# Batch 0's head: both halves' maxima turned, the second sum in its scores' bank, the first products mixed

## The chip, the cores and the metric

The kernel runs on one core of a Trainium2 chip. The metric is the device time of one execution in microseconds (us); a version is told by the median of several runs. Engines are named as in the profile: PE is TensorE's products (PEld its weight loads), DVE is VectorE, ACT is ScalarE, POOL is GpSimd, SP is SyncE, which issues DMAs only.

## What is computed

Two cross attentions between a sequence and a small state, for 8 batches of 8 heads, feed a feed-forward layer with a leaky ReLU.

```python
# x: (8, 8, 512, 64), state: (8, 8, 32, 64)
scores = scale * x @ state.T               # per batch and head: 512 x 32
a = exp(scores - scores.max(-1)); a /= a.sum(-1) + 1e-9
xread = a @ state                          # 512 x 64
scores2 = scale * state @ x.T              # 32 x 512
a2 = exp(scores2 - scores2.max(-1)); a2 /= a2.sum(-1) + 1e-9
sread = a2 @ x                             # 32 x 64
rows = concatenate([xread, sread], axis=2) # per batch 544 rows of 8*64 = 512
h = rows @ w_in                            # 512 x 2048
out = max(0.01 * h, h) @ w_out             # 2048 x 512
```

The sequence rows and the state rows go through the feed-forward layer apart. The sequence part is regrouped: `M = state @ w_in` is formed per batch (256 x 2048: 8 heads of 32 state rows, in two groups of 128 partitions), and the hidden layer is `M.T @ a`, so that xread itself is never formed.

## The kernel before, in words

All loops are unrolled in Python, and each engine executes its instructions in the order in which the code writes them; an engine that waits holds up all that is behind it in its queue. There is no scheduler that moves instructions.

**Tiles.** One core has eight PSUM banks of 128 partitions x 512 fp32. The code names them by tag: `ph` and `py` have two single banks each, `sc` and `big` are one pair of banks each. A tile that is asked for under a tag takes the next buffer of the tag, and its first write waits until the readers of the tile that was there are done.

**Batch 0's head** (lines 490 to 673) is written by hand, because nothing else can fill the engines while the first inputs arrive. Its steps, by the functions that the change touches:

- `spin` (L172): seven idle products on a tile of zeros.
- `x0_t(q)` (L505), q = 0 to 3: batch 0's x, cast by VectorE (L150), is transposed by four products against the identity; ScalarE copies the result to `xT` (L508). For q > 0, `zeros_in` (L498) first puts one 256-column product of zeros into the same bank.
- `scores0(q)` (L519): scores with sequence positions on partitions, 64 columns for each of the four blocks of positions. `max0(q)` (L548, VectorE) takes their maxima over the 32 states, negated.
- A "half" u is four heads. `split0` (L558, L560, VectorE) writes half u's maxima as a sum of two bf16 parts into `parts[u]`.
- `rows0(u)` (L530): the same scores once more, now with (head, state) on partitions and positions on columns, into the tile `scn[u]` under `ph`: four products of 32 output partitions each.
- The negated maxima are added onto `scn[u]` by products. For half 0 `turn0` (L566) turns the 32 columns of parts into 32 rows with one product, ScalarE copies them to `mt` (L571), and `spread_turned` (L576) adds them with four products against a selector. For half 1 `spread0` (L538) spreads each part with 16 products of 32 output partitions, 32 in all, straight from `parts[1]`.
- `exp0(u)` (L583, ScalarE) takes the exponential of `scn[u]`.
- `open_sums` (L589) writes the small constant 1e-9 into both halves' sums, which lie in two banks of one tile under `big`; `sum0(u)` (L596) adds the exponentials over the states with four products; `recip0(u)` (L604, VectorE) takes the reciprocal.
- `recip0_rows(u)` (L538 again) spreads the reciprocals over the state rows with 16 products into a tile `qb0[u]` under `ph`, and `probs0(u)` (L612, VectorE) multiplies: `aT[:, u]`, the probabilities.
- `a_m(a, c, tag)` (L400): one quarter (512 of 2048 columns) of M, 8 products. ScalarE copies out quarter 0 of batch 0 (L670) and of batch 1 (L412), VectorE quarter 1 of both (L414), and for batch 0 quarters 2 and 3 in halves (`m_halves`, L707).

**Batch 0's first products** (L686): for each pair j of the 16 blocks of 128 hidden columns four products, over two groups g and two blocks v, in the order g outside and v inside, into two banks under the tags ph, py, big, ph, py, ph, py, big; ScalarE applies the leaky ReLU (L694, L698). Between pairs stand quarters 2 and 3 of batch 0's M and batch 0's second scores (L264).

**Output products** (`piece`, L449) multiply a block of hidden columns by `w_out`. Batch 0's first ones are interleaved with batch 1's transposes (L743), its scores (L264) and quarters 2 and 3 of its M, which both use the two `ph` banks and are copied out by ScalarE (L412).

After this head, the other batches run in one loop in which TensorE's first products (L421) and output products (L449) alternate.

Of the kernel before, what the change touches and what calls it, by code (L numbers as in the profile page):

```python
# [9 lines left out]
P = 128  # L10
# [17 lines left out]
def kernel(  # L28
# [466 lines left out]

    def zeros_in(flat, n, w):
        for _ in range(n):
            nc.tensor.matmul(flat[:, :w], lhsT=idle[:, :P], rhs=idle[:, :w], start=True, stop=True)  # L498

    def x0_t(q):  # L500
        ps = psum.tile([P, NT, P], FP32, name="pxth", tag=("ph", "py")[q // 2])
        if q:
            zeros_in(ps[:].rearrange("p t c -> p (t c)"), 1, S // 2)
        for t in range(NT):
            nc.tensor.matmul(  # L505
                ps[:, t, :], lhsT=pair_of(a0, t, q), rhs=ident[:], start=True, stop=True
            )
        SCA(a0.xT[:, :, q, :], ps[:])  # L508
# [18 lines left out]
    def rows0(u):  # L527
        scn[u] = psum.tile([P, S], FP32, name="scn", tag="ph")
        for c in range(NK):
            nc.tensor.matmul(  # L530
                scn[u][NS * c:NS * (c + 1), :], lhsT=stbd[:, 2 * u + c // 2, c % 2, :],
                rhs=a0.xT[:, :, 2 * u + c // 2, :], start=True, stop=False,
            )

    def spread0(dst, part, start, stop):
        for t in range(NT):
            for c in range(NK):
                nc.tensor.matmul(  # L538
                    dst[NS * c:NS * (c + 1), P * t:P * (t + 1)],
                    lhsT=part[:, t, c:c + 1].to_broadcast([P, NS]),  # L540
                    rhs=ident[:], start=start, stop=start or (stop and t == NT - 1),
                )
# [20 lines left out]

    def turn0():
        pt = psum.tile([NR, P], FP32, name="pmt", tag="py")
        nc.tensor.matmul(  # L566
            pt[:], lhsT=parts[0][:].rearrange("p t s c -> p (t s c)"), rhs=ident[:],
            start=True, stop=True,
        )
        mt = consts.tile([NR, P], BF16, name="mt")  # L570
        SCA(mt[:], pt[:])  # L571
        return mt

    def spread_turned(dst, mt):
        for t in range(NT):
            nc.tensor.matmul(  # L576
                dst[:, P * t:P * (t + 1)], lhsT=sel[:NR, t].rearrange("r c n -> r (c n)"),
                rhs=mt[:], start=False, stop=t == NT - 1,
            )
# [4 lines left out]

    def open_sums():
        rs = psum.tile([P, 2, S], FP32, name="r0", tag="big", bufs=1)
        for u in range(2):
            r0[u] = rs[:, u, :NG]
            nc.tensor.matmul(  # L589
                r0[u], lhsT=nc.const_aps.tensor(1.0, (2, P), BF16), rhs=eps[:],  # L590
                start=True, stop=False,
            )

# [13 lines left out]
    def recip0_rows(u, q):  # L607
        qb0[u] = psum.tile([P, S], FP32, name="qb0", tag="ph")
        spread0(qb0[u], q[:].rearrange("p (t c) -> p t c", t=NT), True, True)

# [40 lines left out]
    max0(3)  # L651
    mt = turn0()
    rows0(1)
    open_sums()
    split0(m0[1], parts[1][:, :, 0], parts[1][:, :, 1])
    spread_turned(scn[0], mt)
    exp0(0)
    for i in range(2):
        spread0(scn[1], parts[1][:, :, i], False, i == 1)
    exp0(1)  # L660
    pm, pm1 = a_m(a0, 0, "sc"), a_m(a1, 0, "py")
    sum0(0)
    q = [recip0(0)]
    sum0(1)
    q.append(recip0(1))
# [35 lines left out]

    def m_halves(a, c, tag):
        pm = a_m(a, c, tag)
        for i in range(2):
            part = slice(2 * P * i, 2 * P * (i + 1))
            cols = slice(DM * c + 2 * P * i, DM * c + 2 * P * (i + 1))
            VEC(a.M[:, :, cols], pm[:, :, part])  # L707

    for j, tag in enumerate(("ph", "py", "big", "ph", "py", "ph", "py", "big")):
        j *= 2  # L710
        t, bk = open_ff1_0(tag)
        for g in range(2):
            ff1_0(bk, j, g)
        relu0(t, j)
        if j == 4:
            m_halves(a0, 2, "sc")
        elif j == 8:
            a_scores(a0)
            m_halves(a0, 3, "big")
            a_max2(a0)  # L720
# [214 lines left out]
```

## Time and profile before

| | |
|---|---|
| median of 3 runs | 214.61 us (214.38 to 214.87) |
| profiled execution, its own time | 214.58 us |
| its span, first to last instruction | 212.2 us |
| TensorE busy in the span | 205.7 us |
| ScalarE, VectorE, GpSimd busy | 138.4, 99.3, 26.6 us |
| batch 0's first product of the 16 blocks starts | 12.80 us |

The profile is of one execution. A row of the timeline gives the start and the length of a run of equal instructions, the engine, the line of the kernel, the operation, output and inputs by the program's names, the shapes and the count; in brackets stands the idle time of the engine just before, and what ended it. Single durations within such a run overlap, since products are pipelined. The chain of waits follows the work that ended last back from the end, at each step to what released it or to the instruction before it on its engine. A few records of products can be missing, so a count can be one short.

### The profile page before, as it was taken

What the parts mean: (1) busy time and instruction counts of PE and PEld (TensorE: products, weight loads), DVE (VectorE), ACT (ScalarE), POOL (GpSimd) and SP (SyncE); (2) the same over time, 40 slices, a digit from 0 to 9 for tenths busy, and PEclk for the clock granted to TensorE, in tenths of its full rate; (3) what the DMA queues carried; (4) which work ended last, traced back from release to release, by engine and by line L of the source; (5) the groups of instructions that cost most, each with busy time, mean ns of one, the idle gap of its engine ahead of it and who ended that gap; (6) DMA issues with size and microseconds to landing.
All of it is one profiled execution on the core that took longest, in us unless ns stands there. A gap on an engine that the chain in (4) does not pass through costs nothing.

```text
span 212.2 us, 3638 instructions
## 1 busy us (share of the span) xinstructions
PE 205.7 (97%) x1456; PEld 97.0 (46%) x1481; DVE 99.3 (47%) x148; ACT 138.4 (65%) x265; POOL 26.6 (13%) x40
## 2 busy tenths in 40 slices
PE   7989999999999999999999999999999999999994
PEld 2543444343554444444444445444444445466543
DVE  4777795896857055832684096604592000000001
ACT  3679656997787477856686569648884656464420
POOL 8814200030032050530000000000000000000000
PEclk9999999999999999999999999999999999999999
DMA  6999999974973986497117221422115210111123
GB/s 190 208 207 296 255 252 153 314 166 87 246 200 86 209 229 222 100 285 112 49 53 150 50 100 53 109 39 102 49 49 99 88 61 2 49 49 53 49 49 99
DMA packets 38415, 27.68 MB, mean 130 GB/s; under 512 B 24576, under 2 KB 33152, under 8 KB 38400
## 3 DMA queue, kind: packets, MB, share of 16 engines
q1 hardware_dynamic: 32624, 18.75, 34.8%
q0 software_dynamic: 5392, 8.39, 17.9%
q10 hardware_dynamic: 384, 0.33, 0.8%
q8 instruction: 11, 0.18, 0.3%
q14 instruction: 4, 0.03, 0.1%
HBM read 17.30 MB, written 8.91 MB: 124 GB/s over the span
## 4 chain that ended last, share of the span: by engine, by line
PE 94%; DMA 2%; issue 1%; DVE 1%; ACT 0%; DVEq 0%
PE py L449 50%; PE ph L421 23%; PE pm L400 4%; PE ph L432 3%; PE pyw L449 3%; PE ph L686 3%; PE psr L373 2%; DMA xf<-in_x_dram 2%; PE pyh L474 2%; PE sc L264 1%; PE php L686 1%; PE pxth L505 1%; DVE aT L612 0%; PE pxt L743 0%; DVE xb L150 0%
## 5 line engine op out<-in xcount | busy, mean ns | idle before, releaser
L449 PE MATMUL py<-w_out_bf,hT 128*128 128x512 bf16 x445 | 116.7, 379 | 0.9
L426 ACT ACTIVATE hT<-ph 128x512 bf16<-128x512 f32 x112 | 66.4, 601 | 39.1 <-PE ph L421 39.1
L449 PEld LDWEIGHTS <-hT 128*128 128x128 bf16 x496 | 46.9, 98 | 56.9 <-issue 4.9
L421 PE MATMUL ph<-aT,M 128*128 128x512 bf16 x223 | 65.2, 379 | 0.1
L421 PEld LDWEIGHTS <-M 128*128 128x128 bf16 x224 | 21.8, 98 | 27.0 <-issue 1.4
L458 ACT COPY ysb<-py 128x512 f32<-128x512 f32 x31 | 18.1, 585 | 12.3 <-PE py L449 11.6
L274 DVE TRANSPOSE_TENSOR_REDUCE mrow<-sc 128x32 f32<-128x1024 f32 x7 | 8.8, 1250 | 33.9 <-PE sc L264 33.9
L479 DVE COPY ysh<-pyh 128x384 f32<-128x384 f32 x1 | 0.6, 558 | 48.1 <-PE pyh L474 48.1
L143 POOL CAST xb<-xl 128x2048 bf16<-128x2048 f32 x5 | 9.5, 1891 | 55.9 <-DMA xl<-in_x_dram 45.1
L296 DVE TRANSPOSE_TENSOR_REDUCE r<-e 128x32 f32<-128x1024 bf16 x7 | 8.7, 1245 | 11.2 <-ACT e L291 11.2
L414 ACT CAST M<-pm 128x1024 bf16<-128x1024 f32 x11 | 11.1, 1011 | 1.1 <-PE pm L400 0.7
L330 ACT ACTIVATE e<-sc,mcol 128x512 bf16<-128x512 f32 x16 | 11.1, 698 | 0.0
L414 DVE CAST M<-pm 128x1024 bf16<-128x1024 f32 x9 | 10.8, 1216 | 0.0
L324 DVE TENSOR_REDUCE mcol<-sc 128x2 f32<-128x1024 f32 x8 | 9.7, 1215 | 0.0
L436 ACT ACTIVATE hs<-ph 128x256 bf16<-128x256 f32 x16 | 6.0, 385 | 4.6 <-PE ph L432 4.4
L305 DVE STREAM_TRANSPOSE qb<-qh 128x1024 bf16<-128x1024 bf16 x7 | 8.7, 1246 | 0.2
L282 DVE STREAM_TRANSPOSE mrowb<-mrow 128x1024 f32<-128x1024 f32 x7 | 8.7, 1245 | 0.2
L284 DVE TENSOR_TENSOR sh<-sc,mrowb 128x1024 f32<-128x1024 f32 x7 | 8.6, 1225 | 0.2
L432 PE MATMUL ph<-sr_t,w_in_bf 128*128 128x256 bf16 x64 | 8.3, 273 | 0.0
L449 PE MATMUL pyw<-w_out_bf,hT 128*128 128x512 bf16 x30 | 7.8, 379 | 0.1
L400 PE MATMUL pm<-w_in_bf,st_t 64*32 64x512 bf16 x192 | 7.6, 379 | 0.0
L291 ACT ACTIVATE e<-sh 128x1024 bf16<-128x1024 f32 x7 | 7.4, 1053 | 0.3 <-DVE sh L284 0.3
(107 smaller groups left out, 159.2 us busy)
## 6 DMA issues: line engine op xcount, KB each, us to landing
out_dram<-ysb SPq DMA_DIRECT2D x31, 256.0 KB, 2.3
xl<-in_x_dram SPq DMA_DIRECT2D x3, 1024.0 KB, 6.5
w_in_bf<-in_moe_w_in_dram POOLq DMA_DIRECT2D x4, 512.0 KB, 9.4
xl<-in_x_dram POOLq DMA_DIRECT2D x2, 1024.0 KB, 6.4
w_out_bf<-in_moe_w_out_dram POOLq DMA_DIRECT2D x6, 256.0 KB, 12.6
xf<-in_x_dram SPq DMA_DIRECT2D x4, 256.0 KB, 4.0
x<-in_x_dram POOLq DMA_DIRECT2D x2, 512.0 KB, 13.9
xl<-in_x_dram POOLq DMA_DIRECT2D x2, 512.0 KB, 13.8
```

What stands on the lines that cost most here:

```text
L143: nc.gpsimd.tensor_copy(xt[b][:].rearrange("p t h d -> p h t d"), xl[b][:].rearrange("p h (t d) -> p h t d", t=NT),)
L274: nc.vector.tensor_reduce(out=m1[:], in_=flat.rearrange("p (c j) -> p c j", j=NS), axis=AX.X, op=ALU.max, apply_transpose=True,)
L282: nc.vector.transpose(m1b[:], m1[:, :, None].to_broadcast([P, n, NS]))
L324: nc.vector.tensor_reduce(out=a.m2[:], in_=a.sc[:], axis=AX.X, op=ALU.max, negate=True)
L330: nc.scalar.activation(out=a.e2[:, g], in_=a.sc[:, g, :], func=AF.Exp, bias=a.m2[:, g:g + 1], accum_out=a.r2[:, g:g + 1],)
L400: nc.tensor.matmul(at[v][NS * r:NS * (r + 1)], lhsT=st_of(a, g, k), rhs=w_in_bf[D * g:D * (g + 1), k, DM * c:DM * (c + 1)], start=True, st ...
L414: copy(a.M[:, :, cols], pm[:])
L421: nc.tensor.matmul(ph[:], lhsT=a.M[:, g, P * j:P * (j + 1)], rhs=a.aT[:, g, :], start=(g == 0), stop=(g == 1),)
L426: nc.scalar.activation(out=hT[:, j, :], in_=ph[:], func=AF.Prelu, scale=1 / SCALE, alpha=0.01)
L432: nc.tensor.matmul(ph[:, :n], lhsT=w_in_bf[:, k, P * j:P * (j + 1)], rhs=sr_t[:, k, :], start=(k == 0), stop=(k == NK - 1),)
L449: nc.tensor.matmul(y.py, lhsT=hT[:, j, P * i:P * (i + 1)], rhs=w_out_bf[:, j, :], start=(j == 0), stop=(j == 15),)
L458: copy(ysb[:], ys[b, i].py)
```

## The change

Four edits, all in batch 0's head and the work just behind it:

1. `zeros_in` and its three products go. `rows0` writes 64 output partitions with each product, two for a half instead of four.
2. Half 1's maxima take the path of half 0's: `turn0(1)` (one product), a copy to a second `mt` tile, by VectorE, and `spread_turned(scn[1], ...)` (four products), in place of 32 products. TensorE does all of this before the sums.
3. The sums are opened one by one. Half 0's is opened and summed, and its reciprocal taken, before M's quarter 0 of batches 0 and 1 (16 products, which stood ahead of it). Half 1's sum is put into `scn[1]`, the bank of the scores that its exponential has read, and comes behind those 16 products.
4. Batch 0's first products are ordered anew: pairs 0 and 2 are opened together, pair 6 has one product ahead of M's quarter 2, the pairs from 8 on go v outside and g inside. Quarter 2 of M is copied out in parts of 128, 128 and 256 columns. Of the output products, the two of row block 3 over the first two hidden blocks go ahead of batch 1's second transposes, and the second two hidden blocks of row block 1 go ahead of batch 1's scores.

In all, TensorE then has 34 products and 34 weight loads fewer. VectorE has two instructions more (the copy and the extra part of quarter 2); the queues of ScalarE, GpSimd and SP keep their order and count.

```diff
-    def zeros_in(flat, n, w):
-        for _ in range(n):
-            nc.tensor.matmul(flat[:, :w], lhsT=idle[:, :P], rhs=idle[:, :w], start=True, stop=True)
-
     def x0_t(q):
         ps = psum.tile([P, NT, P], FP32, name="pxth", tag=("ph", "py")[q // 2])
-        if q:
-            zeros_in(ps[:].rearrange("p t c -> p (t c)"), 1, S // 2)
...
     def rows0(u):
         scn[u] = psum.tile([P, S], FP32, name="scn", tag="ph")
-        for c in range(NK):
+        for v in range(2):
             nc.tensor.matmul(
-                scn[u][NS * c:NS * (c + 1), :], lhsT=stbd[:, 2 * u + c // 2, c % 2, :],
-                rhs=a0.xT[:, :, 2 * u + c // 2, :], start=True, stop=False,
+                scn[u][D * v:D * (v + 1), :],
+                lhsT=stbd[:, 2 * u + v].rearrange("p g n -> p (g n)"),
+                rhs=a0.xT[:, :, 2 * u + v, :], start=True, stop=False,
             )
...
-    def turn0():
+    def turn0(u, copy):
         pt = psum.tile([NR, P], FP32, name="pmt", tag="py")
         nc.tensor.matmul(
-            pt[:], lhsT=parts[0][:].rearrange("p t s c -> p (t s c)"), rhs=ident[:],
+            pt[:], lhsT=parts[u][:].rearrange("p t s c -> p (t s c)"), rhs=ident[:],
             start=True, stop=True,
         )
-        mt = consts.tile([NR, P], BF16, name="mt")
-        SCA(mt[:], pt[:])
+        mt = consts.tile([NR, P], BF16, name=f"mt{u}")
+        copy(mt[:], pt[:])
         return mt
...
-    def open_sums():
-        rs = psum.tile([P, 2, S], FP32, name="r0", tag="big", bufs=1)
-        for u in range(2):
-            r0[u] = rs[:, u, :NG]
-            nc.tensor.matmul(
-                r0[u], lhsT=nc.const_aps.tensor(1.0, (2, P), BF16), rhs=eps[:],
-                start=True, stop=False,
-            )
+    def open_sum(u, bank):
+        r0[u] = bank[:, :NG]
+        nc.tensor.matmul(
+            r0[u], lhsT=nc.const_aps.tensor(1.0, (2, P), BF16), rhs=eps[:],
+            start=True, stop=False,
+        )
...
-    mt = turn0()
+    mt = [turn0(0, SCA)]
     rows0(1)
-    open_sums()
     split0(m0[1], parts[1][:, :, 0], parts[1][:, :, 1])
-    spread_turned(scn[0], mt)
+    spread_turned(scn[0], mt[0])
     exp0(0)
-    for i in range(2):
-        spread0(scn[1], parts[1][:, :, i], False, i == 1)
+    mt.append(turn0(1, VEC))
+    spread_turned(scn[1], mt[1])
     exp0(1)
-    pm, pm1 = a_m(a0, 0, "sc"), a_m(a1, 0, "py")
+    open_sum(0, psum.tile([P, 2, S], FP32, name="r0", tag="big", bufs=1)[:, 0])
     sum0(0)
     q = [recip0(0)]
+    pm, pm1 = a_m(a0, 0, "sc"), a_m(a1, 0, "py")
+    open_sum(1, scn[1])
     sum0(1)
     q.append(recip0(1))
...
-    def m_halves(a, c, tag):
+    def m_parts(a, c, tag, at):
         pm = a_m(a, c, tag)
-        for i in range(2):
-            part = slice(2 * P * i, 2 * P * (i + 1))
-            cols = slice(DM * c + 2 * P * i, DM * c + 2 * P * (i + 1))
+        for i in range(len(at) - 1):
+            part = slice(at[i], at[i + 1])
+            cols = slice(DM * c + at[i], DM * c + at[i + 1])
             VEC(a.M[:, :, cols], pm[:, :, part])
...
-    for j, tag in enumerate(("ph", "py", "big", "ph", "py", "ph", "py", "big")):
-        j *= 2
+    t0, b0 = open_ff1_0("ph")
+    t2, b2 = open_ff1_0("py")
+    ff1_0(b0, 0, 0, (0,))
+    ff1_0(b2, 2, 0)
+    ff1_0(b0, 0, 0, (1,))
+    ff1_0(b0, 0, 1)
+    ff1_0(b2, 2, 1)
+    relu0(t0, 0)
+    relu0(t2, 2)
+    t4, b4 = open_ff1_0("big")
+    for g in range(2):
+        ff1_0(b4, 4, g)
+    relu0(t4, 4)
+    t6, b6 = open_ff1_0("ph")
+    ff1_0(b6, 6, 0, (0,))
+    m_parts(a0, 2, "sc", (0, P, 2 * P, DM))
+    ff1_0(b6, 6, 1, (0,))
+    for g in range(2):
+        ff1_0(b6, 6, g, (1,))
+    relu0(t6, 6)
+    for j, tag in ((8, "py"), (10, "ph"), (12, "py"), (14, "big")):
         t, bk = open_ff1_0(tag)
-        for g in range(2):
-            ff1_0(bk, j, g)
+        for v in range(2):
+            for g in range(2):
+                ff1_0(bk, j, g, (v,))
...
     for u in range(2):
-        if u:
-            piece(0, h0, 2, 0, bank=wide[:, 0], js=half[0])
-        else:
-            for i in range(2):
+        for i in range(2):
+            if u:
+                piece(0, h0, 2 + i, 0, bank=wide[:, i], js=half[0])
+            else:
                 piece(0, h0, i, 0, js=half[0])
...
-    piece(0, h0, 3, 0, bank=wide[:, 1], js=half[0])
-    piece(0, h0, 0, 0, js=half[1])
+    for i in (0, 1):
+        piece(0, h0, i, 0, js=half[1])
     a_scores(a1)
     m_evict(a1, 2, a_m(a1, 2, "ph"), SCA)
...
-    for i in range(1, NT):
+    for i in (2, 3):
         piece(0, h0, i, 0, js=half[1])
```

More of the change, by code (lines that the diff above doesn't have):

```diff
@@ L528, in rows0, with spread0 @@
         scn[u] = psum.tile([P, S], FP32, name="scn", tag="ph")
-        for c in range(NK):
+        for v in range(2):
             nc.tensor.matmul(
-                scn[u][NS * c:NS * (c + 1), :], lhsT=stbd[:, 2 * u + c // 2, c % 2, :],
-                rhs=a0.xT[:, :, 2 * u + c // 2, :], start=True, stop=False,
+                scn[u][D * v:D * (v + 1), :],
+                lhsT=stbd[:, 2 * u + v].rearrange("p g n -> p (g n)"),
+                rhs=a0.xT[:, :, 2 * u + v, :], start=True, stop=False,
             )
-    def spread0(dst, part, start, stop):
+    def spread0(dst, part):
         for t in range(NT):
@@ L540, in spread0 @@
                     lhsT=part[:, t, c:c + 1].to_broadcast([P, NS]),
-                    rhs=ident[:], start=start, stop=start or (stop and t == NT - 1),
+                    rhs=ident[:], start=True, stop=True,
                 )
@@ L608, in recip0_rows @@
         qb0[u] = psum.tile([P, S], FP32, name="qb0", tag="ph")
-        spread0(qb0[u], q[:].rearrange("p (t c) -> p t c", t=NT), True, True)
+        spread0(qb0[u], q[:].rearrange("p (t c) -> p t c", t=NT))
     def probs0(u):
@@ L700, in relu0 @@
             )
-    def m_halves(a, c, tag):
+    def m_parts(a, c, tag, at):
         pm = a_m(a, c, tag)
-        for i in range(2):
-            part = slice(2 * P * i, 2 * P * (i + 1))
-            cols = slice(DM * c + 2 * P * i, DM * c + 2 * P * (i + 1))
+        for i in range(len(at) - 1):
+            part = slice(at[i], at[i + 1])
+            cols = slice(DM * c + at[i], DM * c + at[i + 1])
             VEC(a.M[:, :, cols], pm[:, :, part])
-    for j, tag in enumerate(("ph", "py", "big", "ph", "py", "ph", "py", "big")):
-        j *= 2
+    t0, b0 = open_ff1_0("ph")
[19 more added lines that the diff above has]
+    for j, tag in ((8, "py"), (10, "ph"), (12, "py"), (14, "big")):
         t, bk = open_ff1_0(tag)
-        for g in range(2):
-            ff1_0(bk, j, g)
+        for v in range(2):
+            for g in range(2):
+                ff1_0(bk, j, g, (v,))
         relu0(t, j)
-        if j == 4:
-            m_halves(a0, 2, "sc")
-        elif j == 8:
+        if j == 8:
             a_scores(a0)
-            m_halves(a0, 3, "big")
+            m_parts(a0, 3, "big", (0, 2 * P, DM))
             a_max2(a0)
```

## The prediction, made before the change was run

> **What bounds the kernel now.** The page comes first.
>
> ```profile
> span 212.2 us, 3638 instructions
> PE 205.7 (97%) x1456; PEld 97.0 (46%) x1481; DVE 99.3 (47%) x148; ACT 138.4 (65%) x265; POOL 26.6 (13%) x40
> PE 94%; DMA 2%; issue 1%; DVE 1%; ACT 0%; DVEq 0%
> ```
>
> TensorE is busy 97% of the span and carries 94% of the chain that ended last. So whatever makes TensorE stand still once, or start its long stream later, is paid at the end in full. The stream becomes dense at batch 0's first products, about 13.4 us in. The edits lie before that point and, for one pair of output products, near 25 us. The chain of waits through the head says what leads there:
>
> ```profile
> 5.74 0.21 PE pxth L498
> ...
> 6.81 0.21 PE pxth L498
> ...
> 9.66 0.56 PE scn L538 x32
> 10.22 0.56 PE pm L400 x16
> ```
>
> Columns: start, length, what. Nearly all the removed work (the fillers L498, the 32-fold spread L538) stands on this chain, so at first sight it looks like a gain of most of a microsecond. But a chain step on TensorE is only what TensorE did last before the next thing; whether something else was due at the same time has to be read from the order in time, engine by engine:
>
> ```profile
> 7.49 0.76 DVE L548 TENSOR_REDUCE m<-sct 128x8 f32<-128x256 f32 x2 [0.23 <-PE sct L519]
> ...
> 8.49 0.17 DVE L560 TENSOR_TENSOR parts<-m,parts 128x16 bf16<-128x16 f32 x1
> 8.58 0.75 DVE L548 TENSOR_REDUCE m<-scq 128x8 f32<-128x256 f32 x2
> ...
> 9.57 0.17 DVE L560 TENSOR_TENSOR parts<-m,parts 128x16 bf16<-128x16 f32 x1
> ...
> 11.59 0.26 DVE L604 RECIPROCAL q<-r 128x16 bf16<-128x16 f32 x1 [0.33 <-PE r L596]
> 12.02 1.29 DVE L612 TENSOR_TENSOR aT<-e,qb 128x512 bf16<-128x512 bf16 x2 [0.17 <-PE qb L538]
> 13.22 2.35 DVE L414 CAST M<-pm 128x1024 bf16<-128x1024 f32 x2
> ```
>
> Columns: start, length, engine, line, operation, tiles, count, and in brackets the idle time before it. From 7.49 to 9.74 no row notes idle time after the first: VectorE, not TensorE, decides when half 0's maxima (8.49 + 0.17 = 8.66) and half 1's (9.57 + 0.17 = 9.74) stand ready as parts.
>
> **The fillers and the wider score rows: nothing.**
>
> ```profile
> 5.13 0.61 PE L505 MATMUL pxth<-ident,xb 128*128 128x128 bf16 x4 [0.32 <-DVE xb L150]
> ...
> 6.42 0.40 PE L519 MATMUL sct<-stbd,xT 128*128 128x64 bf16 x4
> 7.16 0.29 PE L519 MATMUL sct<-stbd,xT 128*128 128x64 bf16 x4
> 7.39 0.39 PE L505 MATMUL pxth<-ident,xb 128*128 128x128 bf16 x4
> 8.49 0.29 PE L519 MATMUL scq<-stbd,xT 128*128 128x64 bf16 x4
> 8.71 0.23 PE L566 MATMUL pmt<-ident,parts 128*32 128x128 bf16 x1
> ...
> 9.29 0.38 PE L576 MATMUL scn<-mt,sel 32*128 32x128 bf16 x4
> ...
> 11.31 0.24 PE L596 MATMUL r<-zeroed,e 128*128 128x4 bf16 x4 [0.35 <-DVE q L604]
> ```
>
> Without the fillers the third transposes can be earlier by their 0.21 us, and the last score block (8.49 to 8.78) by about 0.1; but the reduction that reads it begins only as VectorE comes to it, at about 8.9. The reductions themselves start on the scores of 7.16, which wait for a ScalarE copy and not for a filler. The two 64-column products in place of four 32-column ones lie between the best case (side by side, one 0.22 pace as four take now) and one after the other (0.22 more); either ends ahead of the turned maxima, for which the four products of 9.29 wait (ScalarE's copy, 8.98 + 0.26 = 9.24, below). Cover gone, each would cost those 0.1 to 0.2 us. I take 0.
>
> **Half 1's maxima, turned instead of spread.** For half 0 the trace shows this whole path.
>
> ```profile
> 8.98 0.26 ACT L571 CAST mt<-pmt 32x128 bf16<-32x128 f32 x1 [0.58 <-PE pmt L566]
> 9.70 1.17 ACT L583 ACTIVATE e<-scn 128x512 bf16<-128x512 f32 x2 [0.47 <-PE scn L576]
> 11.71 1.10 ACT L412 CAST M<-pm 128x512 bf16<-128x512 f32 x2
> ```
>
> Parts ready at 8.66, exponential begun at 9.70: 1.04 us for a product, a copy, four products and the handovers. Half 1's copy goes to VectorE, and no row has VectorE copying 128 columns out of PSUM. Bounds: 0.26 (the reciprocal of 16 columns above) and 0.38 (half of the 0.76 of two reductions of 256). I take 0.29, near the lower, for 128 columns lie between; so 1.07. Half 1's exponential then starts at 9.74 + 1.07 = 10.81 and ends at 11.41. Today the two exponentials end together at 9.70 + 1.17 = 10.87. So half 1's is 0.54 us *later*: the spread was short (0.56 on the chain) and overlapped half 0's exponential, while the turned path is latency. Behind it on ScalarE wait the four M copies, which slide by the same 0.54: the last ends at 12.81 + 0.54 = 13.35.
>
> **Sums.** Today the second sum stands behind the first reciprocal: it starts at 11.31 after 0.35 of idle time, though its exponentials were ready at 10.87. In its own bank that wait goes, and it now waits for 11.41. Opening it (one small product into the bank that the exponential has just left) and getting into the sum's shape costs between 0.04 and 0.2; I take 0.16 with the handover, so 11.57. Behind the opener in TensorE's queue stand the second sum and the spreads of both reciprocals, half 0's too, and VectorE's two products of aT wait for those. From a sum's start to its reciprocal's end takes 11.85 − 11.31 = 0.54 today, hence 12.11 against 11.85: **0.26 later**. The first M quarter's 16 products (0.56) move behind the first sum; they run while half 1's exponential is under way, so they cost nothing, and if that cover were gone they would cost 0.56. The second opener moves along and no DMA does; SP's and GpSimd's queues stay in order.
>
> [...]
>
> **First products mixed.**
>
> ```profile
> 11.90 0.18 PEld L538 LDWEIGHTS <-q 128*32 128x32 bf16 x12 [0.19 <-DVE q L604]
> 12.80 0.39 PE L686 MATMUL ph<-aT,M 128*128 128x512 bf16 x1
> 13.36 1.67 PE L686 MATMUL ph<-aT,M 128*128 128x512 bf16 x6 [0.17 <-DVE aT L612]
> 14.87 1.03 PE L686 MATMUL php<-aT,M 128*128 128x512 bf16 x4
> ```
>
> From half 1's reciprocal on (11.85, with 0.05 of handover), TensorE runs through: spread 11.90, M quarter 1, first product 12.80. The second product needs the bank that aT's last step frees at 13.31, so TensorE loses 13.36 − 12.80 − 0.22 = **0.34**. In the changed order everything is 0.26 later: first product 13.06, two of pair 2 at 13.28 and 13.49 (their banks were copied out by 13.35), then half 0's other at 13.71, when aT (13.31 + 0.26 = 13.57) is long there. The 0.34 is gone. The pair read from the third pair of blocks is then due at 14.87 + 0.26 − 0.34 = 14.79; M quarter 1 is cast by 13.22 + 2.35/2 + 0.26 = 14.66, so it just fits. The first of quarter 2's narrower casts (a quarter of such a cast, 0.3, to the 0.38 above) has three products (0.65) ahead of its reader. The head: **−0.08 us**.
>
> **The output products moved.** Row block 3's two go ahead of batch 1's second transposes, and in their place row block 1's two come from behind batch 1's M quarter 2 to ahead of its scores:
>
> ```profile
> 24.58 0.40 PE L400 MATMUL pm<-w_in_bf,st 64*32 64x512 bf16 x8
> 24.91 0.60 PE L449 MATMUL py<-w_out_bf,hT 128*128 128x512 bf16 x2
> 25.35 0.81 PE L449 MATMUL pyw<-w_out_bf,hT 128*128 128x512 bf16 x3
> 26.31 0.41 PE L400 MATMUL pm<-w_in_bf,st 64*32 64x512 bf16 x8
> 25.04 1.07 ACT L412 CAST M<-pm 128x512 bf16<-128x512 f32 x2 [1.27 <-PE pm L400]
> ```
>
> Quarter 3 (26.31) uses the two banks that ScalarE empties by 25.04 + 1.07 = 26.11, that is 1.53 after quarter 2's start, 1.58 with the handover. Today six products (one record missing) fill 1.73. With four left, TensorE is there at 1.73 − 0.43 = 1.30 and waits 1.58 − 1.30 = **0.28**. Bounds: 0, if the first bank alone held it up (its second product needs the second bank, so I exclude it nearly), and 0.35. Batch 1's scores also come 0.43 later, but the work that follows has some 0.9 us before TensorE reads it at 34.6.
>
> ```profile
> 32.95 0.69 DVE L306 TENSOR_TENSOR aT<-e,qb 128x1024 bf16<-128x1024 bf16 x1
> 34.59 0.86 PE ph L421 x4
> ```
>
> **Sum**: −0.08 + 0.28 = +0.20 us on the profiled execution's 214.58 (span 212.2 and 2.4 around it), which is the runs' median 214.61 less 0.03: **214.8**. With the copy, the opener and the stall at their bounds: 214.3 to 215.0. Of this kernel 0.2% (0.43 us) can be told from nothing.
>
> **Rivals.** *The clock comes late* (slower). The four transposes take 0.61 at 5.13 and 0.39 at 7.39: TensorE goes at half pace until about 6.9.
>
> ```profile
> 3.40:6.90 3.50, 3.18 (x26) 1.60 (x25) 2.68 (x5) 1.50 (x4) 3.50 (x5) 1.00 1.10 306
> ```
>
> Columns: stretch, its length, busy time and count on PE, PEld, DVE, ACT and POOL, granted clock, DMA share, GB/s. TensorE is busy 3.18 of these 3.50 us, fillers included (the granted clock reads 1.00 throughout, so only the pace tells). Take 0.4 us of fillers away and full pace may come later. If it lasts past the last score block: 0.11 for the scores at 7.16, 0.22 for the transposes, 0.11 for scores, 0.21 for rows, less some 0.22 in which the block now lies ready or comes earlier: 0.43 more, **215.2**. For it: fillers do nothing else visible. Against: the share falls only by a tenth. [...]
>
> [...]
>
> *The chain is right* (faster): TensorE's count does set the head. Then fillers 0.42 and the spread 0.56 go, 0.23 and 0.38 for turning come back, and with the 0.34 the head gains 0.71; less 0.28 that is 0.43: **214.1**, or 213.9 if the later stall does not come. Against it stands VectorE's unbroken row until 9.74.
>
> *The head changes nothing and the stall does not appear*: 214.5.
>
> **How the numbers follow.** Forecast 0.38 (of it 0.07 beyond +0.43), late clock 0.24 (0.22), dearer path 0.17 (0.16), chain right 0.18 (0.16 at −0.43 or beyond), nothing 0.03. Faster 0.16, same 0.39, slower 0.45: no single case of slower is likelier than the forecast, but they add up. For 8 in 10 the range is 214.0 to 215.5, taking in most of each rival.
>
> **What would show it.** Half 1's exponential starting near 10.8 and its reciprocal ending near 12.1; no idle at the first products; the third pair of blocks' first product at about 14.8; quarter 3 of batch 1 waiting about 0.28 for ScalarE; transposes from 6.9 on still at 0.39 for four. A first M quarter ending before 10.8, or four transposes at 0.6 after 7.3, would prove the sum wrong.

## The result, and the profile after

The changed kernel took **217.11 us** (median of 6 runs, 215.91 to 218.04) against 214.54 (6 runs, 214.22 to 214.87) for the kernel before, measured beside it: ratio **1.0116, 95% interval 1.0075 to 1.0157**. Ratios here leave out runs more than 1.5% above their kernel's fastest, and those are often the very runs that lost the TensorE clock, so the experiments below also give the median over all runs and count the runs whose mean granted clock over the span is under 0.995.

The page of the changed kernel's profiled execution (217.19 us, span and instructions first; then busy time by engine, the granted clock in 40 slices, and the shares of the chain that ended last):

```profile
span 214.8 us, 3596 instructions
PE 209.7 (98%) x1447; PEld 97.6 (45%) x1447; DVE 100.2 (47%) x150; ACT 138.6 (65%) x265; POOL 26.3 (12%) x40
PEclk9979999999999999999999999999999999999999
PE 92%; DVE 4%; DMA 2%; ACT 0%; issue 0%; SPq 0%; ACTq 0%; DVEq 0%
```

TensorE has *fewer* instructions (34 by the code; the records show 1447 products for 1456, since some are missing, and 1447 weight loads for 1481) and is busy 4.0 us *longer* (209.7 for 205.7). More busy time with less work can only be slower work. The third slice of the clock, 10.7 to 16.1 us, shows a 7. Cut at the points where the clock changes (stretch, length, busy time and count on PE, PEld, DVE, ACT and POOL, granted clock, DMA share, GB/s):

```profile
9.77:13.18 3.41, 2.95 (x77) 1.82 (x83) 1.64 (x6) 2.57 (x5) 1.34 (x2) 1.00 1.24 207
13.18:16.59 3.41, 3.41 (x23) 1.05 (x8) 2.98 (x4) 1.05 (x3) 0.70 (x1) 0.50 1.24 207
16.59:20.00 3.41, 3.41 (x22) 1.15 (x20) 1.35 (x3) 3.41 (x8) 1.41 (x2) 1.00 1.10 338
```

The clock was released at 9.77 (before: about 6.9), was taken back for exactly one stretch of 3.41 us from 13.18, and then stayed. Ahead of the first release the column reads 1.00 whatever the pace, so there only the pace tells. TensorE in order of time (start, length, line, operation, tiles, count, and in brackets the idle time before):

```profile
7.35 0.61 PE L499 MATMUL pxth<-ident,xb 128*128 128x128 bf16 x4
...
9.87 0.39 PE L571 MATMUL scn<-mt,sel 32*128 32x128 bf16 x4
10.20 0.23 PE L561 MATMUL pmt<-ident,parts 128*32 128x128 bf16 x1
10.79 0.38 PE L571 MATMUL scn<-mt,sel 32*128 32x128 bf16 x4 [0.37 <-DVE mt L566]
...
13.23 0.68 PE L400 MATMUL pm<-w_in_bf,st 64*32 64x512 bf16 x8
13.84 3.24 PE L680 MATMUL ph<-aT,M 128*128 128x512 bf16 x8
16.92 1.03 PE L680 MATMUL php<-aT,M 128*128 128x512 bf16 x4
```

The transposes at 7.35 still take 0.61 for four, the half pace. The eight first products take 16.92 − 13.84 = 3.08 where 8 × 0.216 = 1.73 were due (0.216 is the median spacing of such products at full clock in this trace): +1.35 in one place. VectorE and ScalarE over the turned path:

```profile
9.90 0.17 DVE L555 TENSOR_TENSOR parts<-m,parts 128x16 bf16<-128x16 f32 x1
10.46 0.28 DVE L566 CAST mt<-pmt 32x128 bf16<-32x128 f32 x1 [0.39 <-PE pmt L561]
...
12.33 0.26 DVE L597 RECIPROCAL q<-scn 128x16 bf16<-128x16 f32 x1 [0.67 <-PE scn L589]
```

```profile
11.21 0.60 ACT L578 ACTIVATE e<-scn 128x512 bf16<-128x512 f32 x1 [0.31 <-PE scn L571]
```

Half 1's parts stand ready at 9.90 + 0.17 = 10.07, against 9.74 before (+0.33); its exponential starts 1.14 later; its reciprocal ends at 12.59.

**Where the time went.** The third pair of blocks starts at 16.92 instead of 14.87, 2.05 later. That is the forecast's own −0.08, plus 0.48 for the reciprocal (12.59 for the forecast 12.11: 0.33 from the late parts, 0.07 in the turned path, 0.08 in the sum), plus 0.30 for half pace on the M products just ahead, the second eight of which take 0.68 here and 0.40 in e4 (first product 13.84 − 12.59 = 1.25 after the reciprocal, for the forecast 13.06 − 12.11 = 0.95), plus 1.35 for half pace on the first products. Then the stall of the output products, first the row of the kernel before that stands behind its quarter 3, then the changed kernel:

```profile
26.65 1.90 PE L449 MATMUL py<-w_out_bf,hT 128*128 128x512 bf16 x8
```

```profile
27.04 0.40 PE L400 MATMUL pm<-w_in_bf,st 64*32 64x512 bf16 x8
27.37 1.04 PE L449 MATMUL pyw<-w_out_bf,hT 128*128 128x512 bf16 x4
28.33 0.69 PE L400 MATMUL pm<-w_in_bf,st 64*32 64x512 bf16 x8
28.96 1.90 PE L449 MATMUL py<-w_out_bf,hT 128*128 128x512 bf16 x8
```

Quarter 3's eight products spread over 0.69 instead of 0.41. From quarter 2's start to the products behind quarter 3 it is 28.96 − 27.04 = 1.92; before, the same stretch held two more products (0.43) and ended at 26.65, 2.07 after 24.58. So 1.92 − (2.07 − 0.43) = **0.28** of waiting.

A last piece comes some 60 us later. VectorE and GpSimd of the kernel before, then of the changed one:

```profile
86.80 0.85 DVE L306 TENSOR_TENSOR aT<-e,qb 128x1024 bf16<-128x1024 bf16 x1
...
89.59 1.29 DVE L412 CAST M<-pm 128x512 bf16<-128x512 f32 x2 [0.82 <-PE pm L400]
```

```profile
85.22 1.89 POOL L143 CAST xb<-xl 128x2048 bf16<-128x2048 f32 x1 [5.54 <-DMA xl<-in_x_dram]
```

```profile
89.10 2.05 DVE L306 TENSOR_TENSOR aT<-e,qb 128x1024 bf16<-128x1024 bf16 x1
...
92.18 1.28 DVE L412 CAST M<-pm 128x512 bf16<-128x512 f32 x2
```

```profile
88.72 1.89 POOL L143 CAST xb<-xl 128x2048 bf16<-128x2048 f32 x1 [6.47 <-PE psr L373]
```

The product of aT starts 2.30 later, as all of TensorE's stream does by then. But GpSimd's cast of x came 3.50 later and now covers the product almost whole: in both kernels the product ends 0.54 after the cast's end (87.65 after 87.11; 91.15 after 90.61), so it now takes 2.05 for 0.85. The 0.82 that VectorE had to spare ahead of its M casts (89.59) is gone, and they start 2.59 later, not 2.30. TensorE loses another 0.2 there; span 214.8 − 212.2 = 2.6. The shift at the head alone does not explain this piece: in e1 the product starts 3.81 later than before and takes 0.75, in e2 0.81 later and takes 1.77. How the cast falls on it differs from one profiled run to the next.

### The profile page after: what moved, and what is told of

It is laid out like the page before. It is cut to its first block, busy times and chain, and to the rows that moved or that the text cites. A ratio compares the mean times of both kernels' runs of the same rounds, so it can differ in the third digit from the quotient of the medians.

```text
span 214.8 us, 3596 instructions
## 1 busy us (share of the span) xinstructions
PE 209.7 (98%) x1447; PEld 97.6 (45%) x1447; DVE 100.2 (47%) x150; ACT 138.6 (65%) x265; POOL 26.3 (12%) x40
## 4 chain that ended last, share of the span: by engine, by line
PE 92%; DVE 4%; DMA 2%; ACT 0%; issue 0%; SPq 0%; ACTq 0%; DVEq 0%
PE py L449 48%; PE ph L421 21%; PE pm L400 4%; PE pyw L449 3%; PE ph L432 3%; PE ph L680 3%; DMA xf<-in_x_dram 2%; PE pyh L474 2%; PE psr L373 2%; PE sc L264 1%; DVE aT L306 1%; PE php L680 1%; PE pxth L499 1%; DVE r L296 1%; DVE qb L305 1%; DVE M L412 1%
## 5 line engine op out<-in xcount | busy, mean ns | idle before, releaser
L449 PE MATMUL py<-w_out_bf,hT 128*128 128x512 bf16 x464 | 119.0, 379 | 0.1
L426 ACT ACTIVATE hT<-ph 128x512 bf16<-128x512 f32 x112 | 66.4, 601 | 41.5 <-PE ph L421 41.5
L688 ACT ACTIVATE hT<-ph 128x512 bf16<-128x512 f32 x12 | 6.2, 621 | 2.5 <-PE ph L680 2.4
```

Of the source, the lines that this page charges most:

```text
L426: nc.scalar.activation(out=hT[:, j, :], in_=ph[:], func=AF.Prelu, scale=1 / SCALE, alpha=0.01)
L449: nc.tensor.matmul(y.py, lhsT=hT[:, j, P * i:P * (i + 1)], rhs=w_out_bf[:, j, :], start=(j == 0), stop=(j == 15),)
```

## The experiments

The numbers of all runs. "Lost" counts runs with a mean granted clock under 0.995; "full" is the median of the others, without those over 217 us, which are put down to a late first release (last column). A late release does not lower the recorded clock: the run of e3 with 217.9 us and 0.999 was profiled, and its release lies at 17.17. The profiled runs of e8 and e11 are of the same kind; for the other runs in this column the late release is inferred from the time and the clock.

| kernel | lost | median, all | full | ratio to before (95%) | late release |
|---|---|---|---|---|---|
| before, beside e1–e4 | 11 of 35 | 214.78 | 214.61 | | 0 |
| before, beside e5–e8 | 7 of 29 | 214.94 | 214.73 | | 0 |
| before, beside e9–e12 | 10 of 31 | 215.20 | 214.69 | | 0 |
| changed, first | 5 of 6 | 217.11 | – | 1.0116 (1.0075–1.0157) | 1 |
| e11 changed again | 7 of 9 | 216.54 | – | 1.0040 (0.9995–1.0086) | 1 |
| e1 changed + early fillers | 11 of 12 | 216.55 | – | 1.0064 (1.0023–1.0106) | 0 |
| e2 before − early fillers | 1 of 12 | 214.95 | 214.71 | 1.0013 (0.9977–1.0049) | 2 |
| e3 changed + late fillers | 1 of 12 | 214.70 | 214.67 | 0.9976 (0.9939–1.0012) | 1 |
| e4 changed + both fillers | 2 of 12 | 214.74 | 214.69 | 0.9992 (0.9954–1.0029) | 0 |
| e5 e3 + old output order | 4 of 6 | 217.68 | – | 1.0120 (1.0079–1.0161) | 2 |
| e6 changed, half 1 spread | 3 of 12 | 215.04 | 214.64 | 0.9991 (0.9958–1.0024) | 0 |
| e7 before, half 1 turned | 9 of 12 | 216.32 | 215.31 | 1.0062 (1.0026–1.0098) | 0 |
| e8 M quarter in the wait | 10 of 12 | 216.79 | – | 1.0074 (1.0035–1.0113) | 1 |
| e9 = e3 again | 5 of 12 | 215.73 | 214.59 | 0.9987 (0.9942–1.0032) | 0 |
| e10 = e5 again | 4 of 12 | 216.11 | 214.30 | 0.9962 (0.9929–0.9995) | 2 |
| e12 spread, fillers, old order | 1 of 12 | 214.44 | 214.34 | 0.9980 (0.9962–0.9998) | 0 |

### Which fillers hold the clock: e1 to e4

The rival of the prediction blamed the three removed fillers among the transposes. e1 puts them back into the changed kernel:

```diff
         ps = psum.tile(..., name="pxth", tag=("ph", "py")[q // 2])
+        if q:
+            zeros_in(ps[:].rearrange("p t c -> p (t c)"), 1, S // 2)
```

> The changed kernel with the three filler products of before put back, nothing else. Clock theory (the fillers alone bring the half-pace spells): full pace from about 6.9 us on, no second half-pace spell, 214.5 to 215.0 us. Order theory (the new order's thin stretch from the turned maxima to the first products lets the clock fall, the fillers only set the first release): first release at about 6.9 but a half-pace spell of 3.4 us at the first products remains, 215.3 to 217. Latency theory (the turned path itself costs the 2.5 us, the clock little): 216.5 or more at full pace.

e2 takes the same lines out of the kernel before and leaves the rest of it alone.

> The kernel before without its three filler products, nothing else. Clock theory: half pace until 9 to 10 us in most runs and a second spell of 3.4 us in some, 215.5 to 218 us. Order theory: late first release only, 214.9 to 215.3 us. Latency theory: 214.4 to 214.7 us, since the fillers stand in waits.

e3 adds to the changed kernel two products of zeros of 256 columns each, between half 1's turning and its adding, where TensorE waits 0.37 for VectorE's copy. They write into a bank that the first sum opens afterwards:

```diff
     mt.append(turn0(1, VEC))
+    rs = psum.tile([P, 2, S], FP32, name="r0", tag="big", bufs=1)
+    zeros_in(rs[:, 1], 2, S // 2)
     spread_turned(scn[1], mt[1])
...
-    open_sum(0, psum.tile([P, 2, S], FP32, name="r0", tag="big", bufs=1)[:, 0])
+    open_sum(0, rs[:, 0])
```

> The changed kernel, still without the early fillers, with two 256-column products of zeros between turning half 1's maxima and adding them, where TensorE waits for VectorE's copy (0.37 us in the changed kernel's trace). Clock theory: the release stays late and the second spell stays in most runs, 216 to 217.5 us. Order theory: the second spell goes, 214.9 to 215.4 us. Latency theory: as the changed kernel, 217 us.

e4 has both edits, e1's and e3's.

> The changed kernel with the early fillers and with those between turning and adding half 1's maxima. Clock and order theory alike: no half-pace spell after 6.9 us, 214.5 to 215.0 us; the predicted sum without clock losses is 214.8. Latency theory: 216.5 or more.

These results follow the order theory, except that e3 came out faster than its 214.9 to 215.4. The early fillers do not decide the loss: with them the changed kernel still lost the clock in 11 of 12 runs, and without them the kernel before lost it in 1 of 12. The cleanest pair is e1 and e4, which differ in the two late fillers alone and ran on the same chip: 11 of 12 lost, 2 of 12 lost, 216.55 and 214.74. (The profiled run of e1 also waited 0.30 and 0.66 us for a quarter of w_in, so its count of runs says more than its profile.) And e4's profiled run shows what the change costs at full clock. TensorE, then VectorE, then ScalarE:

```profile
9.86 0.39 PE L498 MATMUL r<-idle 128*128 128x256 bf16 x2
10.30 0.38 PE L577 MATMUL scn<-mt,sel 32*128 32x128 bf16 x4
...
13.04 1.90 PE L688 MATMUL ph<-aT,M 128*128 128x512 bf16 x8
14.78 1.03 PE L688 MATMUL php<-aT,M 128*128 128x512 bf16 x4
...
24.90 0.40 PE L400 MATMUL pm<-w_in_bf,st 64*32 64x512 bf16 x8
25.23 1.04 PE L449 MATMUL pyw<-w_out_bf,hT 128*128 128x512 bf16 x4
26.20 0.69 PE L400 MATMUL pm<-w_in_bf,st 64*32 64x512 bf16 x8
26.82 1.47 PE L449 MATMUL py<-w_out_bf,hT 128*128 128x512 bf16 x6
```

```profile
9.47 0.17 DVE L561 TENSOR_TENSOR parts<-m,parts 128x16 bf16<-128x16 f32 x1
9.96 0.28 DVE L572 CAST mt<-pmt 32x128 bf16<-32x128 f32 x1 [0.32 <-PE pmt L567]
...
11.84 0.26 DVE L603 RECIPROCAL q<-scn 128x16 bf16<-128x16 f32 x1 [0.67 <-PE scn L595]
```

```profile
10.71 0.60 ACT L584 ACTIVATE e<-scn 128x512 bf16<-128x512 f32 x1 [0.51 <-PE scn L577]
```

The fillers fit into the wait (9.86 + 0.39 = 10.25, the copy ends at 10.24). Exponential 1.07 after the parts (9.64 to 10.71), copy 0.28, reciprocal ended at 12.10, first products without a wait and 1.74 for eight, third pair at 14.78, and the stall again 26.82 − 24.90 = 1.92. Its span is 212.4 against 212.2.

The last column of the table shows what the early fillers are for. Over all experiments, the kernels that have them (before, e1, e4, e7, e12) show a late release in 0 of 143 runs, those without them in 10 of 93 (none of the 12 runs of e6). In the profiled runs the first release lies between 4.29 and 6.91 with them, and between 4.08 and 17.17 without. Such a run costs some 3 us (217.9 for 214.7 in e3). It is too rare to move a median.

### The turned path undone, and done alone: e6 and e7

e6 gives the changed kernel the 32-fold spread of half 1 back (in the form that adds onto the scores), without any filler:

```diff
-    mt.append(turn0(1, VEC))
-    spread_turned(scn[1], mt[1])
+    for i in range(2):
+        spread0(scn[1], parts[1][:, :, i], False, i == 1)
```

> The changed kernel with half 1's maxima spread by 32 products again; the other edits stay, no fillers at all. Turned-path theory (the wait for the copy of half 1's turned maxima is what makes TensorE's work thin enough for the clock to fall): most runs at a mean clock of 0.998 or more, median 214.4 to 215.0. Rival (the sums and M's quarter 0 in their new places, or the missing fillers, make it thin): most runs at 0.992 or less, 216 to 217.5 us.

e7 is the opposite: the kernel before with its fillers, and these two lines turned round, the copy on VectorE.

> The kernel before, fillers and all, with one part of the change alone: half 1's maxima turned, copied by VectorE and added by four products. Turned-path theory: most runs at a mean clock of 0.992 or less, median 215.7 to 217.5. Rival: the clock as before (about a third of the runs below 0.995), and 0.2 to 0.5 us for the later reciprocal, 214.8 to 215.1 at full clock.

Undone alone, the loss goes (3 of 12, 215.04); done alone, it comes (9 of 12, 216.32, ratio 1.0062). In e7's profiled run the clock fell for two stretches, after one with the turned path in it:

```profile
7.70:11.12 3.42, 1.90 (x24) 1.09 (x21) 1.53 (x7) 1.57 (x4) 1.62 (x3) 1.00 1.23 198
11.12:14.53 3.41, 2.40 (x56) 1.22 (x55) 0.74 (x3) 2.05 (x4) 0.78 (x1) 0.50 1.24 206
14.53:17.95 3.42, 3.42 (x26) 1.04 (x23) 3.33 (x4) 0.93 (x3) 1.45 (x2) 0.50 1.24 232
```

That run also waited 1.70 us for a quarter of w_in, so its one profile does not show the turned path by itself; the count over 12 runs does, against 7 of 29 for the kernel before beside it. e6's median lies just above the 214.4 to 215.0 expected, with the clock held in most runs, and e7 came out as expected. Over all experiments the turned path without late fillers lost the clock in 42 of 51 runs (changed, e11, e1, e7, e8), the spread in 33 of 131 (before, e2, e6, e12). For e6, where the clock held in the profiled run, the stretch with the spread in it reads:

```profile
8.44:11.86 3.42, 3.31 (x100) 2.02 (x97) 1.76 (x7) 2.50 (x6) 1.63 (x3) 1.00 1.24 206
```

There are 100 products there, and 77 in the changed kernel's stretch from 9.77.

### Other work in the wait: e8

e8 issues the first M quarter's first eight products between turning and adding, so that real work fills the wait and none is added (the output products stand in the old order, too):

```diff
     mt.append(turn0(1, VEC))
+    pm = a_m(a0, 0, "sc")
     spread_turned(scn[1], mt[1])
...
-    pm, pm1 = a_m(a0, 0, "sc"), a_m(a1, 0, "py")
+    pm1 = a_m(a1, 0, "py")
```

> The changed kernel without fillers, with batch 0's M quarter 0 (8 products) put between turning and adding half 1's maxima, where TensorE waits, and the output products in their order of before. Thin-stretch theory (any work in that wait keeps the clock): most runs at 0.998 or more, median 214.2 to 214.7. Rival (only wide products of 128 by 128 count, the 64 by 32 ones do not): most runs at 0.992 or less, 215.7 to 217.

The expectation missed: 10 of 12 runs lost the clock. Moving work into the wait is not enough. One reading is that the stretch as a whole is as thin as it was, since nothing was added. The rival on record, that 64 by 32 products do not count, forecast the same outcome, and e8 does not tell the two apart. Its profiled run released late, at 17.17, so it does not show a loss behind a release.

### The output products, and e3 once more: e5, e9, e10

e5 is e3 with the output products in their old order:

```diff
-            if u:
-                piece(0, h0, 2 + i, 0, bank=wide[:, i], js=half[0])
...
+        if u:
+            piece(0, h0, 2, 0, bank=wide[:, 0], js=half[0])
...
-    for i in (0, 1):
-        piece(0, h0, i, 0, js=half[1])
+    piece(0, h0, 3, 0, bank=wide[:, 1], js=half[0])
+    piece(0, h0, 0, 0, js=half[1])
```

> The changed kernel with the two late fillers, and with the output products around batch 1's scores in their order of before. Stall theory (the moved output products leave TensorE waiting 0.28 us for ScalarE at batch 1's M quarter 3): runs at full clock are 0.2 to 0.3 us faster than with the late fillers alone (their median there 214.65), so 214.35 to 214.45, and quarter 3's products start without a wait. Rival (the stall is made up for later): 214.6 to 214.7 us.

It missed: 217.68 us with the clock lost in 4 of 6 runs, though nothing ahead of 21 us differs from e3. In its profiled run the clock, released at 4.08, was taken back at 7.49, during the transposes and ahead of the turned path and the late fillers, so a lost run of a kernel without the early fillers need not be the turned path's doing. e3 had run on another chip, so both were repeated side by side, unchanged.

> The changed kernel with the two late fillers once more, now beside the same with the output products in their old order and beside the changed kernel itself, on one chip. The two with late fillers differ only behind 20 us, and the clock is decided before; yet one kept it in 10 of 12 runs and the other in none of 6. [...]

> The changed kernel with the two late fillers and the output products in their old order. [...] Stall theory: its runs at full clock are 0.2 to 0.3 us below those with late fillers alone.

Now 5 of 12 and 4 of 12: how often the clock falls varies from one measurement to the next, and neither e3's 1 of 12 nor e5's 4 of 6 can be taken by itself. Pooled, the late fillers without the early ones leave 14 of 42 lost, against 12 of 15 for the changed kernel. So they help, and do not cure it. At full clock, the pair e9 and e10 prices the output products. TensorE of e9, then of e10:

```profile
24.80 0.40 PE L400 MATMUL pm<-w_in_bf,st 64*32 64x512 bf16 x8
25.13 1.04 PE L449 MATMUL pyw<-w_out_bf,hT 128*128 128x512 bf16 x4
26.10 0.69 PE L400 MATMUL pm<-w_in_bf,st 64*32 64x512 bf16 x8
26.73 1.47 PE L449 MATMUL py<-w_out_bf,hT 128*128 128x512 bf16 x6
```

```profile
24.37 0.40 PE L400 MATMUL pm<-w_in_bf,st 64*32 64x512 bf16 x8
...
26.10 0.41 PE L400 MATMUL pm<-w_in_bf,st 64*32 64x512 bf16 x8
26.44 1.90 PE L449 MATMUL py<-w_out_bf,hT 128*128 128x512 bf16 x8
```

In the old order quarter 3 runs in 0.41 and what follows starts at 26.44; in the new one it takes 0.69 and the rest starts at 26.73: 0.29. The two kernels' full-clock medians differ by the same (214.59 and 214.30), but they are of 7 and 6 runs that spread over more than 1 us each, so the rows are the better evidence.

### The changed kernel beside them: e11

> The changed kernel itself. Thin-stretch theory: at least three quarters of the runs at a mean clock of 0.992 or less, or with a late release, median 215.9 to 217.5 us. [...]

7 of 9 lost, an eighth released late (the profiled one, at 16.94): the first measurement was no accident, though its size is uncertain (1.0040, interval 0.9995 to 1.0086, for 1.0116). What a run takes depends in part on how many stretches of 3.41 it loses: the profiled run of the changed kernel lost one (mean clock 0.992), that of e1 two (0.984).

### What the parts are worth together: e12

e12 keeps what cost nothing or gained (the wider score rows, the second sum in its scores' bank, the mixed first products) and undoes the rest: half 1 spread as in e6, the early fillers as in e1, the output products as in e5.

> The changed kernel with half 1's maxima spread again, the early fillers back and the output products in their old order; of the change stay the wider score rows, the sums opened one by one and the mixed first products. By the sum at full clock: the second sum no longer waits for the first reciprocal (0.35 us of idle time before) and the 0.34 at the first products goes, with no stall later, so 213.9 to 214.3 us at full clock, and a clock that falls in at most a third of the runs.

214.44 us, the lowest of all: ratio 0.998, interval 0.9962 to 0.9998, with the clock lost in 1 of 12. The interval ends only just below 1, and the ratio of one kernel moved from 1.0120 (e5) to 0.9962 (e10) between two measurements, so the gain is not certain. At full clock it is 214.34 for 214.69, 0.35 less, a little above the 213.9 to 214.3 expected. TensorE and VectorE of its profiled run:

```profile
9.23 0.63 PE L539 MATMUL scn<-ident,parts 128*32 128x128 bf16 x32
...
12.49 1.90 PE L686 MATMUL ph<-aT,M 128*128 128x512 bf16 x8
14.22 1.03 PE L686 MATMUL php<-aT,M 128*128 128x512 bf16 x4
```

```profile
11.20 0.26 DVE L603 RECIPROCAL q<-scn 128x16 bf16<-128x16 f32 x1 [0.67 <-PE scn L595]
```

From the second reciprocal's end (11.46) to the third pair it takes 2.76; before, 14.87 − 11.85 = 3.02. The mixed order gains 0.26 here; in e4 the same stretch takes 14.78 − 12.10 = 2.68, the whole 0.34. The third pair is 14.87 − 14.22 = 0.65 earlier than before, and the full-clock medians show 0.35 of it; where the rest goes was not followed.

## Why the prediction was wrong

The range ended at 215.5; the result lies above it. Step by step:

- *The chain through the head is not what sets it; VectorE's row is*: held. With the clock there, taking the spread off gained nothing (e4, which has the early fillers again: span 212.4; e9, which does not: 212.3; before: 212.2), so the rival "the chain is right" fell.
- *The fillers and the wider score rows, nothing*: held for the fillers in the median (e2's full-clock median is 214.71 for 214.61), but their price was missed: without them some one run in ten (10 of 93) shows a late release. The wider rows were not tried alone.
- *Half 1's latency*: 1.07 forecast, 1.07 in e4 and 1.14 in the changed kernel's profile; VectorE's copy 0.28 for 0.29. So the dearer path, to which the chances give 0.17, did not come.
- *Sums*: the reciprocal 1.30 after the exponential's start by the forecast, 1.39 in e4 (12.10 − 10.71). No row of the kernel before shows the opener's 0.16 of the forecast, taken between 0.04 and 0.2; in e4 the second sum starts 11.47 − 11.31 = 0.16 after the exponential's end, so it held. The missing 0.09 lies between that sum's start and the reciprocal's end, 12.10 − 11.47 = 0.63 for 0.54. By luck e4's parts came 0.10 earlier than in the kernel before and hid it.
- *First products mixed*: no wait, third pair at 14.78 in e4 for 14.79.
- *The output products*: 0.28 forecast, 0.28 in the changed kernel, 0.29 between e9 and e10.
- *The sum*: no run at full clock contradicts it, but at this size they cannot confirm it. The forecast was +0.20; against the kernel before beside them the full-clock medians of e4, e3 and e9, which all have the late fillers, differ by +0.08, +0.06 and −0.10, and the profiled spans of e4 and e9 by +0.2 and +0.1.
- *The clock comes late*: half right. Release did come later, at 9.77, and cost the +0.33 at the parts that this rival had priced at 0.43. That the fillers guard the first release is borne out by the late ones, 0 of 143 and 10 of 93. But this is the smaller and rarer cost. The one that sets the median comes behind the release, and there e1 and e2 show that the early fillers do not decide; e6 and e7 show that half 1's path does.

**The step that failed** is "Half 1's maxima, turned instead of spread". It priced 32 small products against five and a copy as latency alone, 0.54 at the exponential. Shown by e6 and e7: with the turned path the clock also falls again, after it was released, in most runs, and then the eight first products run at half pace: +1.35 there and +0.30 just ahead, 1.65 of the 2.6 in the profiled run. The prediction looked for the clock at the first release and nowhere behind it, and it weighed the fillers by their share of busy time. The second thing it did not have is the +0.2 at 93 us: a cast on GpSimd covers a product on VectorE that it only touched before. Why that cast slid by 3.50 where the rest slid by 2.30 was not tried, and by e1 and e2 the shift alone does not decide it.

What exactly makes the clock fall was not tested by itself. It is not the busy share of the profile, and not the longest wait: the clock stayed after these two stretches, the first of the kernel before, the second of e9 (with TensorE's longest wait in it).

```profile
10.33:13.74 3.41, 2.87 (x74) 1.31 (x60) 2.24 (x5) 2.49 (x5) 0.99 (x2) 1.00 1.25 210
4.38:7.80 3.42, 2.43 (x36) 1.53 (x36) 3.34 (x6) 2.35 (x6) 3.42 (x6) 1.00 1.16 266
5.12 0.40 PE L503 MATMUL pxth<-ident,xb 128*128 128x128 bf16 x4 [0.45 <-DVE xb L150]
```

Both are less busy than the 2.95 of 3.41 us after which the changed kernel lost the clock, and e9's stretch has a wait of 0.45 in one piece where the changed kernel's longest was 0.37. Another count fits the traces better. Take each product's columns, times the size of its weights as a share of the largest in the rows, 128*128 (an eighth for 64*32, a quarter for 128*32 and for 32*128; a product across a boundary counts in part). Add this up over the stretches of 3.41 us that the changes of the clock mark off, carried back in the same steps ahead of the first release. These sums are estimates from the rows:

| run, stretch | TensorE busy | columns, by share of 128*128 | clock in the next stretch |
|---|---|---|---|
| before, 10.33 to 13.74 | 2.87 | 3740 | full |
| changed, 9.77 to 13.18 | 2.95 | 2820 | half |
| e1, 8.87 to 12.29 | 2.53 | 2100 | half |
| e4, 9.00 to 12.42 | 3.15 | 2880 | full |
| e6, 8.44 to 11.86 | 3.31 | 3700 | full |
| e7, 7.70 to 11.12 | 1.90 | 1090 | half |
| e9, 4.38 to 7.80 | 2.43 | 3060 | full |

Of the 63 stretches that end by 19 us in the 14 profiled runs, 62 fall on the right side of a line between 2850 and 2880: below it the clock fell or stayed at half, above it the clock came or stayed. The exception is e1's from 12.29 to 15.70, with 2980 and half pace behind it. Columns counted without that share leave 13 on the wrong side. By this count half 1's spread is worth 32 × 32 = 1024 columns, the turned path 32 + 4 × 32 = 160, the late fillers 512, the early ones 768, and e8's moved products add nothing to the stretch, which is in line with the counts of lost runs. The count was fitted to these traces afterwards and no run was made to test it, so it is argued, not shown.

## What to carry to other kernels

Small products ahead of a dense stream may be what keeps TensorE's clock, even where they are wasteful as arithmetic (here it was lost in 33 of 131 runs with the spread, in 42 of 51 with the turned path and no late fillers): before removing them, read the granted clock in windows behind the first release too, and price the dense stream behind at half pace (here 3.08 for 1.73 us on eight products). TensorE's busy share does not warn of it (2.95 of 3.41 us was lost, 2.43 kept); the count of columns by the size of the weights may, which is argued from these traces alone. The same holds of products of zeros that seem to do nothing: their worth may be a rare run (a late release in 0 of 143 runs with the early fillers, in 10 of 93 without). Compare full-clock medians and the share of runs that lost the clock, not one median, and repeat the count, since it varies between measurements. The overlap of VectorE and GpSimd far behind the edit also differed between profiled runs (the product of aT took 2.05 us in the changed kernel's, 1.12 in e4's, 0.69 in e12's), so read it in several of them before putting it down to the change.

## What was not expected of the hardware

**The clock fell after its release, without a long pause.** It was released at 9.77, and taken back at 13.18 after 3.41 us in which TensorE's longest wait was 0.37. Idle time alone does not decide it here, since e9 kept the clock after a stretch with more of it (3.42 − 2.43 = 0.99 for 3.41 − 2.95 = 0.46).

**The spells have one length and no fixed place.** Half-pace spells in the traces last 3.41 us or a multiple of it (e7: 11.12 to 17.95, e5: 7.49 to 17.73). First releases in the profiled runs lie anywhere from 4.08 (e5) over 9.77 (changed) to 17.17 (e3, e8), and the kernel before lost the clock in 28 of its 95 runs.

**VectorE's product of aT ended half a microsecond after GpSimd's cast where the two overlapped.** Clear of the cast the product takes 0.69 us (the kernel before at 32.95; e12, where it starts at 88.00, 1.73 after the cast's end). Where the cast of x was still running as it started, it took 0.85 (before), 0.88 (e9), 1.12 (e4) and 2.05 (changed), and in each of these four profiled runs it ended 0.53 or 0.54 after the cast. The runs show the overlap and the longer product; what makes the one wait for the other they do not show.
